# A first MLP matmul split into four full 128-row chunks and a paired half-array remainder, with the bias in the gelu

## The chip, the cores and the metric

The kernel runs on one core of one Trainium2 chip. The metric is device time in microseconds (us), of which lower is better. Before the change it was 450.98 us, the median of two runs (450.38 and 451.58).

Names: PE is TensorE, ACT is ScalarE, DVE is VectorE, POOL is GpSimd. A *tile* is 128 of the 2048 token rows, so there are 16. A *stage* is the first MLP matmul of one tile. The *pace* is the distance between the first matmuls of two successive stages, read from the timeline.

## The reference, cut to what matters

```python
# x: 2048 x 576, bf16; w1: 576 x 4608; w2: 4608 x 576
h  = x + attention(layernorm(x)) @ wo             # sliding, dilated, 8 keys a row
y  = layernorm(layernorm(h))
out = h + gelu(y @ w1 + b1) @ w2 + b2             # approximate (tanh) gelu
```

576 channels are four and a half blocks of 128. The change is about that half block.

## The kernel before

A front projects all 16 tiles to q, k, v; then, tile by tile, attention (mostly DVE), output projection (`pw`), layernorm, first MLP matmul (`pm`), gelu (ACT) and second MLP matmul (`po`) run as a pipeline. The first MLP uses five row blocks. The fifth holds the last 64 channels and, at row 64, the bias, met by a column of ones in the activations:

```python
ps_qkv = ... bufs=2, PSUM     # pq and pw
ps_m1  = ... bufs=3, PSUM     # pm: one bank is 4 blocks of 128 outputs, x 128 tokens, f32
# w1_sb[0:64, 4] = w1[512:576];  w1_sb[64, 4] = b1;  hn[:, 576] = 1, hn[:, 577:640] = 0
for g in range(g0, g1):                           # 9 groups a tile, one bank each
    pm = ps_m1.tile([P, GF, P], F32, tag="pm")
    for j in range(GF):
        ft = g * GF + j
        for kt in range(5):
            matmul(pm[:, j, :], lhsT=w1_sb[:, kt, ft*P:(ft+1)*P], rhs=hnT[:, kt, :], ...)
    nc.scalar.activation(out=hTg[:], in_=pm[:], func=Gelu_apprx_tanh)   # 128 x 512
# per iteration: E(it-2); G(it-3, 28..36); loads; F(it-2, first two thirds); C(it-1);
#                F(it-2, rest); D(it-1); G(it-2, 0..28); attention(it)
#                E: transposes hn; F: first MLP; C: transposes o; D: pw, layernorm; G: second MLP
```

The order of the source is not the order on the engines: the tile framework orders the instructions when it builds the program.

## Time and profile before

| stretch | what bounds it |
|---|---|
| 0 to 97 us | front: PE 94% busy and DMA share 0.96 from 56 to 90 us |
| 97 to 263 us | stages start 20.65 to 27.7 us apart; waits on attention and on ACT |
| 263 to 451 us | PE is full; one tile every 20.65 us |

From the page of the kernel before: engine totals, small DMA packets, the chain that ended last by engine, and two groups of instructions (count, busy us, mean ns of one, then idle time before and what ended it):

```profile
PE 408.3 (91%) x4752; PEld 338.5 (75%) x4752; DVE 293.5 (65%) x475; ACT 196.8 (44%) x307; POOL 49.2 (11%) x73
...
DMA packets 56072, 69.32 MB, mean 154 GB/s; under 512 B 2762, under 2 KB 53194, under 8 KB 55896
...
PE 58%; DVE 23%; issue 3%; ACT 2%; POOL 2%; DMA 1%; DVEq 0%; SPq 0%; ACTq 0%; POOLq 0%
...
L328 PE MATMUL pm<-hnT,w_sb 128*128 128x128 bf16 x2880 | 171.8, 222 | 10.1 <-ACT hTg L331 9.3
...
L331 ACT ACTIVATE hTg<-pm 128x512 bf16<-128x512 f32 x144 | 83.4, 598 | 65.5 <-PE pm L328 64.5
```

The gelu is 144 instructions of 598 ns and waits for PE. PE's 9.3 us of waiting for it all lie in the early tiles; from 263 us on there is none. The chain of waits in order of time (start, duration, what) in the late part of the kernel before holds only PE, and repeats every 20.65 us:

```profile
283.84 6.70 PE pm L328 x120
290.82 3.35 PE pm L328 x60
294.17 1.23 PE pw L299 x10
```

One such stage in the timeline of the kernel before (start, duration, engine, line, what; in brackets how long the engine had been idle and what ended that):

```profile
345.63 6.86 PE L328 MATMUL pm<-hnT,w_sb 128*128 128x128 bf16 x120
347.00 1.28 ACT L331 ACT_TABLE_LOAD   x1 [2.43 <-PE pm L328]
348.29 1.58 ACT L331 ACTIVATE hTg<-pm 128x512 bf16<-128x512 f32 x3
350.36 0.60 ACT L331 ACTIVATE hTg<-pm 128x512 bf16<-128x512 f32 x1 [0.50 <-PE pm L328]
...
352.61 3.51 PE L328 MATMUL pm<-hnT,w_sb 128*128 128x128 bf16 x60
...
355.96 1.39 PE L299 MATMUL pw<-wo_sb,oT 128*128 128x432 bf16 x10
```

From 345.63 to 355.96 PE never stops: 180 matmuls and five transposes, 55.8 ns from start to start (the 222 ns of the group is the modelled length of one pipelined matmul, not its cost). ACT is idle about half a microsecond before most gelus.

### The profile page before, as it was taken

To read this page: it belongs to the slowest core of one execution; us is meant where nothing else is said; L and a number is where in the kernel's file an instruction comes from. 1 tells how busy PE (TensorE), PEld (TensorE's weight loads), DVE (VectorE), ACT (ScalarE), POOL (GpSimd) and SP (SyncE) were. 2 spreads that over 40 slices of the span, in tenths; PEclk is the share of its full clock that TensorE was granted. 3 is DMA by queue.
4 is the path that set the end of the run, shared out by engine and by line. 5 is a ranking of instruction groups with operands and counts; after the bars stand their busy time and mean duration, and the time that the engine had idled before them with its cause. 6 is when DMAs were issued, how large, how long until landed. Compare 5 with 4: busy or idle time off the path is not lost.

```text
span 450.8 us, 10955 instructions
## 1 busy us (share of the span) xinstructions
PE 408.3 (91%) x4752; PEld 338.5 (75%) x4752; DVE 293.5 (65%) x475; ACT 196.8 (44%) x307; POOL 49.2 (11%) x73
## 2 busy tenths in 40 slices
PE   0898699849989996999878999999999999999996
PEld 0454355449878986798757898989898998989895
DVE  5835834941788998889997989787879772020200
ACT  5556366524272535072535443536263543324140
POOL 4310001010101010201030101010101101010100
PEclk9999699959999997999998999999999999999999
DMA  8497599999934735534734635334452000000000
GB/s 253 153 261 282 131 309 298 344 348 379 329 107 134 237 119 171 196 118 137 237 120 132 202 112 175 120 132 121 132 157 81 28 15 16 15 1 15 1 16 13
DMA packets 56072, 69.32 MB, mean 154 GB/s; under 512 B 2762, under 2 KB 53194, under 8 KB 55896
## 3 DMA queue, kind: packets, MB, share of 16 engines
q1 hardware_dynamic: 56024, 68.63, 47.7%
q8 instruction: 37, 0.61, 0.6%
q14 instruction: 11, 0.09, 0.1%
HBM read 59.13 MB, written 9.49 MB: 152 GB/s over the span
## 4 chain that ended last, share of the span: by engine, by line
PE 58%; DVE 23%; issue 3%; ACT 2%; POOL 2%; DMA 1%; DVEq 0%; SPq 0%; ACTq 0%; POOLq 0%
PE pm L328 26%; PE pq L203 5%; DVE prod L249 3%; PE pw L299 3%; DVE prod L252 2%; POOL ln_rstd L158 2%; DMA kw_758<-qkvd 1%; DVE prod L253 1%; DVE h L301 1%; PE po_1_6379 L347 1%; PE po_1_6028 L347 1%; PE po_0_5676 L347 1%; PE po_1_4955 L347 1%; PE po_0_4593 L347 1%; PE po_0_4232 L347 1%
## 5 line engine op out<-in xcount | busy, mean ns | idle before, releaser
L328 PE MATMUL pm<-hnT,w_sb 128*128 128x128 bf16 x2880 | 171.8, 222 | 10.1 <-ACT hTg L331 9.3
L328 PEld LDWEIGHTS <-w_sb 128*128 128x128 bf16 x2880 | 168.4, 100 | 12.3 <-issue 11.4
L347 PEld LDWEIGHTS <-hTg 128*128 128x128 bf16 x1152 | 111.7, 98 | 27.0
L331 ACT ACTIVATE hTg<-pm 128x512 bf16<-128x512 f32 x144 | 83.4, 598 | 65.5 <-PE pm L328 64.5
L203 PE MATMUL pq<-wqkv_sb,xnT 128*128 128x432 bf16 x320 | 65.8, 363 | 7.6 <-ACT qkv L205 6.8
L203 PEld LDWEIGHTS <-xnT 128*128 128x128 bf16 x320 | 31.8, 102 | 35.3 <-issue 11.8
L305 POOL TENSOR_TENSOR hb<-h,b_bc 128x576 bf16<-128x576 f32 x16 | 22.5, 1404 | 295.9 <-DVE h L301 295.9
L205 ACT CAST qkv<-pq 128x432 bf16<-128x432 f32 x64 | 32.9, 519 | 26.2 <-PE pq L203 20.6
L301 DVE TENSOR_TENSOR h<-pw,xr 128x432 f32<-128x432 f32 (+1 forms) x32 | 13.1, 450 | 41.9 <-PE pw L299 41.9
L166 ACT COPY hnT<-hnT_pt 128x640 bf16<-128x640 bf16 x16 | 11.0, 690 | 65.0 <-PE hnT_pt L165 65.0
L264 ACT ACTIVATE logits<-logits 128x256 f32<-128x256 f32 x16 | 6.7, 416 | 58.5 <-DVE logits L262 54.6
L158 POOL TENSOR_TENSOR ln_rstd<-ln_veps,mhalf 128x1 f32<-128x1 f32 x32 | 22.2, 694 | 69.7 <-DVE ln_veps L156 69.7
L331 ACT ACT_TABLE_LOAD x15 | 19.2, 1283 | 17.6 <-PE pm L328 17.5
L152 DVE BATCH_NORM_STATS2 ln_stats<-x_bf 128x6 f32<-128x288 bf16 x32 | 13.1, 446 | 17.4 <-DMA x_bf<-in_A_x_dram 17.3
L299 PE MATMUL pw<-wo_sb,oT 128*128 128x432 bf16 (+1 forms) x160 | 22.8, 290 | 1.0 <-ACT oT L166 0.9
L252 DVE TENSOR_TENSOR prod<-prod 128x2304 bf16<-128x2304 bf16 x16 | 22.4, 1400 | 0.4
L299 PEld LDWEIGHTS <-oT 128*128 128x128 bf16 x160 | 13.4, 99 | 8.5 <-ACT oT L166 1.4
L264 ACT ACT_TABLE_LOAD x14 | 18.0, 1283 | 2.0 <-DVE logits L262 1.8
L266 DVE TENSOR_REDUCE den<-logits 128x32 f32<-128x256 f32 x16 | 9.4, 588 | 10.6 <-ACT logits L264 10.6
L165 PE MATMUL xnT_pt<-ident,xn_84 128*128 128x128 bf16 x40 | 4.1, 242 | 11.8 <-DVE xn_84 L159 11.8
L165 PEld LDWEIGHTS <-xn_84 128*128 128x128 bf16 x40 | 3.2, 109 | 13.2 <-DVE xn_84 L159 11.8
L152 DVE BATCH_NORM_STATS2 ln_stats<-h 128x6 f32<-128x288 f32 x32 | 12.9, 447 | 0.0
(193 smaller groups left out, 589.9 us busy)
## 6 DMA issues: line engine op xcount, KB each, us to landing
w_sb<-in_B_w_dram SPq DMA_DIRECT2D x18, 576.0 KB, 8.1
qkvd<-qkv SPq DMA_DIRECT2D x16, 432.0 KB, 3.6
x_bf<-in_A_x_dram SPq DMA_DIRECT2D x16, 144.0 KB, 4.3
xr<-in_A_x_dram SPq DMA_DIRECT2D x16, 144.0 KB, 3.4
q<-qkvd SPq DMA_DIRECT2D x16, 144.0 KB, 4.9
out_dram<-o_sb SPq DMA_DIRECT2D x16, 144.0 KB, 1.7
wraw<-in_A_wqkv_dram SPq DMA_DIRECT2D x4, 432.0 KB, 3.5
kw_285<-qkvd SPq DMA_DIRECT2D x2, 576.0 KB
```

The source lines that it names most:

```text
L152: nc.vector.bn_stats(out=stats[:, c, :], in_=src[:, c * HALF:(c + 1) * HALF])
L158: nc.gpsimd.tensor_tensor(out=rstd[:], in0=veps[:], in1=mhalf[:], op=ALU.pow)
L203: nc.tensor.matmul(pq[:], lhsT=xnT[:, kt, :], rhs=wqkv_sb[:, kt, nq * QC:(nq + 1) * QC], start=(kt == 0), stop=(kt == KT - 1))
L205: nc.scalar.copy(out=qkv[:, nq * QC:(nq + 1) * QC], in_=pq[:])
L252: nc.vector.tensor_tensor(out=pv[:, :, 0:9, :], in0=pv[:, :, 0:9, :], in1=pv[:, :, 9:18, :], op=ALU.add)
L264: nc.scalar.activation(out=logits[:], in_=logits[:], func=ACT.Exp, scale=SCALE)
L299: nc.tensor.matmul(pw[:, 0:c1 - c0], lhsT=oT[:, kt, :], rhs=wo_sb[:, kt, c0:c1], start=(kt == 0), stop=(kt == KT - 1))
L301: nc.vector.tensor_tensor(out=h[:, c0:c1], in0=pw[:, 0:c1 - c0], in1=xr[:, c0:c1], op=ALU.add)
L305: nc.gpsimd.tensor_tensor(out=hb[:], in0=h[:], in1=b2_bc[:], op=ALU.add)
L328: nc.tensor.matmul(pm[:, j, :], lhsT=w1_sb[:, kt, ft * P:(ft + 1) * P], rhs=hnT[:, kt, :], start=(kt == 0), stop=(kt == KT - 1))
L331: nc.scalar.activation(out=hTg[:], in_=pm[:], func=ACT.Gelu_apprx_tanh)
L347: nc.tensor.matmul(po2[half][:], lhsT=hT[g][:, j, :], rhs=w2_sb[:, ft, half * HALF:(half + 1) * HALF], start=(ft == 0), stop=(ft == FT - 1))
```

## The change

The intent is to stop paying 36 full-array matmuls a tile for blocks that are half empty. The remaining 64 channels of two output blocks (`ft` and `ft + 18`) sit on partitions 0 to 63 and 64 to 127 and run side by side in the two halves of the array: 18 slots instead of 36. No row is left for the bias, so it becomes a per-partition operand of the gelu, which then needs one instruction for each 128-wide block. Halves that run together write to different banks (the Trainium skill, "TensorEngine Tiling (Array Packing)", section "Restrictions and Gotchas", says that different row tiles cannot use one PSUM bank at once), so a group now takes two of the three `pm` banks. The core of the diff, with cuts marked:

```diff
-    w1_sb = wpool.tile([P, KT, F], BF16, name="w1_sb")
+    w1_sb = wpool.tile([P, 4, F], BF16, name="w1_sb")
+    w1h_sb = wpool.tile([P, F2], BF16, name="w1h_sb")       # rows 512..575, two halves of F
+    b1_sb = wpool.tile([P, FT], F32, name="b1_sb")
+            nc.sync.dma_start(out=b1_bf[:], in_=B_b1.rearrange("(ft p) -> p ft", p=P))
+        nc.gpsimd.tensor_copy(out=b1_sb[:], in_=b1_bf[:])
     (w1 in 6 loads instead of 8; the double layernorm's eps folded in; hn's last 64 columns copied)
-            pm = ps_m1.tile([P, GF, P], F32, tag="pm", name="pm")
-            (4 blocks x 5 matmuls)
-            nc.scalar.activation(out=hTg[:], in_=pm[:], func=ACT.Gelu_apprx_tanh)
+            pms = [ps_m1.tile([P, GF, P], F32, tag="pm", name=f"pm{r}") for r in range(2)]
+            for j in range(n):
+                for r in range(2):
+                    matmul(pms[r][:, j, :], lhsT=w1h_sb[r*64:(r+1)*64, fa*P:(fa+1)*P],
+                           rhs=hnT[r*64:(r+1)*64, 4, :], start=(j == 0), stop=False, ...)
+            for r in range(2):
+                (4 blocks x 4 full matmuls into pms[r])
+            for r in range(2):
+                for j in range(GF):
+                    nc.scalar.activation(out=hTg[:, j, :], in_=pms[r][:, j, :],
+                                         func=ACT.Gelu_apprx_tanh, bias=b1_sb[:, ft:ft + 1])
```

More of the change, by code (lines that the diff above doesn't have):

```diff
@@ L41 @@
     FT = F // P
+    KC = 9
+    F2 = F // 2
+    FT2 = FT // 2
     NQ = 4
@@ L48 @@
     NG = FT // GF
+    NG2 = (FT2 + GF - 1) // GF
     LSK = 4
@@ L66 @@
     wo_sb = wpool.tile([P, KT, D], BF16, name="wo_sb")
-    w1_sb = wpool.tile([P, KT, F], BF16, name="w1_sb")
+    w1_sb = wpool.tile([P, 4, F], BF16, name="w1_sb")
+    w1h_sb = wpool.tile([P, F2], BF16, name="w1h_sb")
+    b1_bf = wpool.tile([P, FT], BF16, name="b1_bf")
+    b1_sb = wpool.tile([P, FT], F32, name="b1_sb")
     w2_sb = wpool.tile([P, FT, D], BF16, name="w2_sb")
@@ L127, in wo_load @@
         nc.sync.dma_start(out=wo_sb[64:128, KT - 1, :], in_=A_wo[0:64, :])
-    W1C = 8
+    W1C = 6
     CW = F // W1C
     def w1_chunk(c):
-        src = bass.AP(tensor=B_w1.tensor, offset=B_w1[0, c * CW].offset,
-                      ap=[[F, P], [P * F, 4], [1, CW]])
-        nc.sync.dma_start(out=w1_sb[:, 0:4, c * CW:(c + 1) * CW], in_=src)
+        w = F // W1C
+        src = bass.AP(tensor=B_w1.tensor, offset=B_w1[0, c * w].offset,
+                      ap=[[F, P], [P * F, 4], [1, w]])
+        nc.sync.dma_start(out=w1_sb[:, :, c * w:(c + 1) * w], in_=src)
     def w1_blk4():
-        nc.sync.dma_start(out=w1_sb[0:64, 4, :], in_=B_w1[512:576, :])
-        nc.sync.dma_start(out=w1_sb[64:65, 4, :], in_=B_b1.rearrange("(o f) -> o f", o=1))
-        nc.sync.dma_start(out=w1_sb[65:128, 4, :], in_=B_w1[0:63, :])
+        with nc.allow_non_contiguous_dma(reason="bias column layout"):
+            nc.sync.dma_start(out=b1_bf[:], in_=B_b1.rearrange("(ft p) -> p ft", p=P))
+        nc.gpsimd.tensor_copy(out=b1_sb[:], in_=b1_bf[:])
+        for r in range(2):
+            nc.sync.dma_start(out=w1h_sb[r * 64:(r + 1) * 64, :], in_=B_w1[512:576, r * F2:(r + 1) * F2])
     W2C = 9
@@ L155, in layernorm_to @@
         veps = pool.tile([P, 1], F32, tag=f"{tagp}_veps", name=f"{tagp}_veps")
-        nc.vector.tensor_scalar_add(out=veps[:], in0=mv[:, 1:2], scalar1=EPS)
+        if tagp == "ln2":
+            nc.vector.tensor_scalar(out=veps[:], in0=mv[:, 1:2], scalar1=1.0 + EPS, scalar2=EPS * EPS,
+                                    op0=ALU.mult, op1=ALU.add)
+        else:
+            nc.vector.tensor_scalar_add(out=veps[:], in0=mv[:, 1:2], scalar1=EPS)
         rstd = pool.tile([P, 1], F32, tag=f"{tagp}_rstd", name=f"{tagp}_rstd")
         nc.gpsimd.tensor_tensor(out=rstd[:], in0=veps[:], in1=mhalf[:], op=ALU.pow)
-        nc.vector.tensor_scalar(out=dst_bf[:, 0:D], in0=src, scalar1=mv[:, 0:1], scalar2=rstd[:, 0:1],
-                                op0=ALU.subtract, op1=ALU.mult)
+        if tagp == "ln2":
+            nc.vector.tensor_scalar(out=dst_bf[:, 0:D], in0=src, scalar1=mv[:, 0:1], scalar2=rstd[:, 0:1],
+                                    op0=ALU.subtract, op1=ALU.mult)
+            nc.vector.tensor_scalar(out=dst_bf[:, D:DP], in0=src[:, 512:D], scalar1=mv[:, 0:1],
+                                    scalar2=rstd[:, 0:1], op0=ALU.subtract, op1=ALU.mult)
+        else:
+            nc.vector.tensor_scalar(out=dst_bf[:, 0:D], in0=src, scalar1=mv[:, 0:1], scalar2=rstd[:, 0:1],
+                                    op0=ALU.subtract, op1=ALU.mult)
     def transpose_to(dstT, src_bf, tagp):
@@ L323, in stage_F @@
         for g in range(g0, g1):
-            pm = ps_m1.tile([P, GF, P], F32, tag="pm", name="pm")
-            for j in range(GF):
-                ft = g * GF + j
-                for kt in range(KT):
-                    nc.tensor.matmul(pm[:, j, :], lhsT=w1_sb[:, kt, ft * P:(ft + 1) * P], rhs=hnT[:, kt, :],
-                                     start=(kt == 0), stop=(kt == KT - 1))
-            hTg = sb.tile([P, GF, P], BF16, tag="hT", name="hTg", bufs=10)
-            nc.scalar.activation(out=hTg[:], in_=pm[:], func=ACT.Gelu_apprx_tanh)
-            d["hT"].append(hTg)
-        if g1 == NG:
+            pms = [ps_m1.tile([P, GF, P], F32, tag="pm", name=f"pm{r}") for r in range(2)]
+            n = min(GF, FT2 - g * GF)
+            for j in range(n):
+                fa = g * GF + j
+                for r in range(2):
+                    nc.tensor.matmul(pms[r][:, j, :], lhsT=w1h_sb[r * 64:(r + 1) * 64, fa * P:(fa + 1) * P],
+                                     rhs=hnT[r * 64:(r + 1) * 64, 4, :], start=(j == 0), stop=False,
+                                     skip_group_check=True)
+            for r in range(2):
+                for j in range(n):
+                    ft = r * FT2 + g * GF + j
+                    for kt in range(4):
+                        nc.tensor.matmul(pms[r][:, j, :], lhsT=w1_sb[:, kt, ft * P:(ft + 1) * P],
+                                         rhs=hnT[:, kt, :], start=False, stop=(kt == 3), skip_group_check=True)
+            for r in range(2):
+                hTg = sb.tile([P, GF, P], BF16, tag="hT", name="hTg", bufs=10)
+                for j in range(GF):
+                    fa = g * GF + j
+                    if fa >= FT2:
+                        break
+                    ft = r * FT2 + fa
+                    nc.scalar.activation(out=hTg[:, j, :], in_=pms[r][:, j, :], func=ACT.Gelu_apprx_tanh,
+                                         bias=b1_sb[:, ft:ft + 1])
+                    d["hT"].append((hTg, j, ft))
+        if g1 == NG2:
             d.pop("hnT")
@@ L344, in stage_G @@
         for ft in range(f0, f1):
-            g, j = ft // GF, ft % GF
+            hTg, j, fx = hT[ft]
             for half in range(2):
-                nc.tensor.matmul(po2[half][:], lhsT=hT[g][:, j, :], rhs=w2_sb[:, ft, half * HALF:(half + 1) * HALF],
+                nc.tensor.matmul(po2[half][:], lhsT=hTg[:, j, :], rhs=w2_sb[:, fx, half * HALF:(half + 1) * HALF],
                                  start=(ft == 0), stop=(ft == FT - 1))
@@ L366 @@
         nc.gpsimd.memset(o_slots[j][:, D:DP], 0.0)
-        nc.gpsimd.memset(hn_slots[j][:, D:D + 1], 1.0)
-        nc.gpsimd.memset(hn_slots[j][:, D + 1:DP], 0.0)
     emit_misc_setup()
@@ L396 @@
             pending.append((k, fn))
-    post = [lambda: w1_chunk(6), lambda: w1_chunk(7)] + [lambda c=c: w2_chunk(c) for c in range(W2C)] \
+    post = [lambda c=c: w2_chunk(c) for c in range(W2C)] \
         + [lambda: loads(2)]
@@ L420 @@
             loads(it + 1)
-        stage_F(it - 2, 0, 6)
+        stage_F(it - 2, 0, 3)
         stage_C(it - 1)
-        stage_F(it - 2, 6, NG)
+        stage_F(it - 2, 3, NG2)
         stage_D(it - 1)
```

## The prediction

> **What bounds the kernel now.** Three stretches. (1) Up to 97 us: the projection of all 16 tiles plus loading; the stretch table shows DMA share 0.96 from 56 to 90 us and 1.06 from 90 to 112 us. (2) From 97 us (first pm matmul) to about 247 us, MLP tiles start 20.7 to 27.8 us apart, the chain of waits mostly in VectorE's attention. (3) From 247 us on TensorE is full: the chain holds only PE, one tile every 20.65 us: 180 first-MLP matmuls (120 in 6.70 us, so 55.9 ns each, 10.05 us). The gelu there is cheap: the timeline shows 9 ACTIVATEs of 128x512 per tile, 598 ns each (0.49 us apart back to back).
>
> **What the change does.**
> - TensorE: 36 of the 180 matmuls of a tile become 36 half-array ones. If a pair shares one slot, 18 slots are saved: 18 x 55.9 ns = 1.0 us a tile, 16 us in all. That is an upper bound: the trace cannot show whether pairs overlap or what going from half to full array and back costs.
> - ScalarE: per tile 36 ACTIVATEs of 128x128 with a bias pointer replace 9 of 128x512 without. From the trace's 432, 512 and 640 wide PSUM reads (519, 598, 690 ns) the slope is about 0.83 ns an element, so a 128-wide one is about 280 ns; the Trainium skill, "ScalarE: Activation LUTs", section "What ACT_TABLE_LOAD costs", adds about 93 ns for each pointer operand (not in this trace). About 370 ns long, some 0.26 to 0.29 us apart: 9.4 to 10.6 us a tile against 4.5 to 5.4.
> - That lands inside the first-MLP stage. Only three pm banks exist, and now a group takes two, so group g+1 cannot start before the gelus of the bank it takes are done. ACT starts about 2.1 us after the stage's first matmul (table load 1.28 us after its first block) and must finish seven of ten banks before the last group runs. Estimate: 2.1 + 28 x 0.27 + 0.6 + about 1.2 = 11.5 us for the stage, against 10.05 + 0.44 (oT transposes) now. So the stage becomes ACT-bound and grows by about 1 us a tile (0 to 2), instead of shrinking by 1: about +17 us over 16 tiles.
> - Loading: the bias goes into columns, 4608 two-byte elements; by the Trainium skill, "DMA: Bandwidth & Descriptors", "Rules for kernel authors", a strided last dimension is one descriptor per element. At this trace's mean 61 ns a packet (47.7% of 16 engines' span over 56024 packets), 288 per engine take about 18 us of a busy queue, with qkv stores behind them. Idle DMA time (share 0.51 from 45 to 56 us) absorbs part. Estimate: +7 us before the first MLP matmul.
>
> **Predicted time:** 474 us, 8 in 10 between 450 and 498. Faster by over 2%: 0.07; within 2%: 0.20; slower by over 2%: 0.73.
>
> **What would show each step.** Gelu group about 370 ns x576; "PE pm waits for ACT hTg" growing from 9.3 us to 20 or more; tile pace after 250 us about 21.7 us instead of 20.65; half matmuls under 56 ns apart; over 4000 more small packets and a later first pm matmul.
>
> **What would make it wrong.** If the bias pointer costs nothing, ACT keeps pace and the pace falls to about 20 us: then 440 to 450. If pairs don't overlap, more is lost. The order around the early tiles' exp may change too.

## The result, and the profile after

The changed kernel took 470.1 us (median of 469.85 and 470.35) against 450.98: ratio 1.0431, 95% interval 1.0385 to 1.0476. A ratio here is the mean time of one kernel's fast runs over that of the other's of the same rounds, so it is not quite the ratio of the medians quoted.

The same parts of the page of the changed kernel:

```profile
PE 426.8 (91%) x4752; PEld 328.8 (70%) x4752; DVE 297.4 (64%) x491; ACT 267.0 (57%) x739; POOL 48.4 (10%) x70
...
DMA packets 59650, 68.77 MB, mean 147 GB/s; under 512 B 7360, under 2 KB 56768, under 8 KB 59598
...
PE 55%; DVE 12%; ACT 11%; issue 3%; POOL 2%; DVEq 0%; ACTq 0%; POOLq 0%
```

ACT went from 196.8 to 267.0 us busy and from 2% to 11% of the chain. The count of matmuls did not fall: 36 full ones a tile became 36 half ones. The late part of the chain, where before there was only PE:

```profile
309.56 1.01 PE pm_4620 L356 x16
310.64 1.28 ACT L365
312.20 0.89 ACT hTg L365 x3
313.51 1.00 PE pm_4673 L356 x16
315.66 0.62 PE pm_4724 L356 x9
316.37 1.15 ACT hTg L365 x4
317.94 1.00 PE pm_4784 L356 x16
318.94 0.89 PE pm_4785 L356 x16
321.44 1.23 PE pw L319 x10
```

Within one stage the chain now goes from PE to ACT and back: a bank of matmuls, the table load and gelus, the matmuls that could take the freed bank, gelus again. One group of the narrow gelus by its source line (count, then shortest, median and longest ns):

```profile
L365 ACT ACTIVATE hTg<-pm_1101,b_sb x4: 361/368/377, 101.5 to 102.3; 128x128 bf16<-128x128 f32 x4
```

And a stage in the timeline of the changed kernel:

```profile
354.24 0.23 PE L349 MATMUL pm_5402<-hnT,w1h_sb 64*128 64x128 bf16 x1
354.24 0.23 PE L349 MATMUL pm_5403<-hnT,w1h_sb 64*128 64x128 bf16 x1
354.30 0.22 PE L349 MATMUL pm_5402<-hnT,w1h_sb 64*128 64x128 bf16 x1
354.31 0.22 PE L349 MATMUL pm_5403<-hnT,w1h_sb 64*128 64x128 bf16 x1
...
354.42 0.22 PE L349 MATMUL pm_5403<-hnT,w1h_sb 64*128 64x128 bf16 x1
...
354.57 1.07 PE L356 MATMUL pm_5402<-hnT,w_sb 128*128 128x128 bf16 x16
...
356.46 0.39 PE L349 MATMUL pm_5454<-hnT,w1h_sb 64*128 64x128 bf16 x4
...
357.01 1.14 ACT L365 ACTIVATE hTg<-pm_5402,b_sb 128x128 bf16<-128x128 f32 x4
...
358.03 1.16 ACT L365 ACTIVATE hTg<-pm_5403,b_sb 128x128 bf16<-128x128 f32 x4
...
362.91 0.21 PE L349 MATMUL pm_5567<-hnT,w1h_sb 64*128 64x128 bf16 x1 [0.41 <-ACT hTg L365]
```

Three things are to be seen. Two halves start together (both at 354.24, the next pair 0.06 us later): pairs do share a slot. Between the last half (354.42) and the first full matmul (354.57) there are 0.15 us, not 0.06. And at 356.46 four halves of one bank run alone, although the source writes them in pairs, so there are more changes between half and full array than the source has. The builder placed them so; e4 and e11 below show why.

Where the 17.3 us between the two profiled spans (450.8 and 468.1) lie, by stage starts: the first stage begins at 97.73 us instead of 97.26 (+0.5); the ninth at 286.62 instead of 283.68 (+2.5 more over eight tiles, which had slack to give); the last at 443.98 instead of 428.25 (+12.8 over seven tiles); the rest is the tail (+1.6).

All start-to-start distances of a late stage, from its first matmul to the first `pw` matmul, can be sorted into four kinds. A full matmul or transpose costs 56 ns. A *trip* is a change from full to half array (152 ns start to start) and back (148 ns); what exceeds 56 ns there counts as "changes". What exceeds the usual distance is "wait". ("Full" is the count times 56 ns, so the row of the kernel before is 0.03 above its measured stage.) The same sum for the experiments below is in the table already, since it is what they are read by (us a tile):

| kernel | full | halves | changes | wait | stage | pace |
|---|---|---|---|---|---|---|
| before | 10.36 | - | - | 0 | 10.33 | 20.65 |
| changed | 8.34 | 1.75 | 1.41 | 0.62 | 12.12 | 22.54 |
| e1: one wide gelu per bank, no bias | 8.34 | 1.29 | 1.03 | 0.14 | 10.80 | 21.22 |
| e2: narrow gelus, no bias pointer | 8.34 | 1.40 | 1.03 | 0.23 | 11.01 | 21.42 |
| e3: before, with narrow gelus and pointer | 10.36 | - | - | 0.47 | 10.82 | 21.15 |
| e4: changed, five banks | 8.34 | 1.08 | 0.84 | 0.03 | 10.29 | 20.71 |
| e8: five banks, wide gelu, 3 trips | 8.34 | 1.05 | 0.47 | 0.01 | 9.87 | 20.29 |

The change saves 2.02 us of full matmuls a tile. Ideally the halves need 1.08 of that back; they take 1.75 because pairs are apart (of the 288 pairs in the whole trace, 61 start within 10 ns of each other; the expectation of e11 counts 207 as apart, so 81 together). Changes take 1.41 and waits 0.62. So PE loses in three ways, only one of them a visible wait. The question for the experiments is what makes the two others: the order as such, the narrow gelus, or the banks.

### The profile page after: what moved, and what is told of

It reads as the page before. It is cut to its first block, busy times and chain, and to the rows that moved or that the text cites. A ratio compares the mean times of both kernels' runs of the same rounds, so it can differ in the third digit from the quotient of the medians.

```text
span 468.1 us, 11416 instructions
## 1 busy us (share of the span) xinstructions
PE 426.8 (91%) x4752; PEld 328.8 (70%) x4752; DVE 297.4 (64%) x491; ACT 267.0 (57%) x739; POOL 48.4 (10%) x70
## 2 busy tenths in 40 slices
DMA packets 59650, 68.77 MB, mean 147 GB/s; under 512 B 7360, under 2 KB 56768, under 8 KB 59598
## 4 chain that ended last, share of the span: by engine, by line
PE 55%; DVE 12%; ACT 11%; issue 3%; POOL 2%; DVEq 0%; ACTq 0%; POOLq 0%
ACT hTg L365 7%; PE pw L319 4%; ACT L365 3%; DVE prod L269 2%; PE pq L223 2%; POOL ln_rstd L172 1%; DVE prod L272 1%; PE po_0_3719 L382 1%; PE po_0_6827 L382 1%; PE po_1_6447 L382 1%; PE po_0_5674 L382 1%; PE po_1_5284 L382 1%; PE po_0_4892 L382 1%; PE po_1_4502 L382 1%; PE po_1_4111 L382 1%
## 5 line engine op out<-in xcount | busy, mean ns | idle before, releaser
L356 PEld LDWEIGHTS <-w_sb 128*128 128x128 bf16 x2304 | 130.7, 98 | 13.0 <-issue 0.2
L223 PE MATMUL pq<-wqkv_sb,xnT 128*128 128x432 bf16 x320 | 65.6, 362 | 11.0 <-ACT qkv L225 10.3
L349 PEld LDWEIGHTS <-w1h_sb 64*128 64x128 bf16 x576 | 28.4, 94 | 24.8 <-issue 12.4
L272 DVE TENSOR_TENSOR prod<-prod 128x2304 bf16<-128x2304 bf16 x16 | 21.7, 1356 | 0.4
L162 DVE BATCH_NORM_STATS2 ln_stats<-x_bf 128x6 f32<-128x288 bf16 x32 | 13.4, 446 | 12.4 <-DMA x_bf<-in_A_x_dram 12.4
L273 DVE TENSOR_TENSOR prod<-prod 128x1024 bf16<-128x1024 bf16 x16 | 11.8, 735 | 0.4
```

Source lines behind the costliest of these rows:

```text
L162: nc.vector.bn_stats(out=stats[:, c, :], in_=src[:, c * HALF:(c + 1) * HALF])
L223: nc.tensor.matmul(pq[:], lhsT=xnT[:, kt, :], rhs=wqkv_sb[:, kt, nq * QC:(nq + 1) * QC], start=(kt == 0), stop=(kt == KT - 1))
L272: nc.vector.tensor_tensor(out=pv[:, :, 0:9, :], in0=pv[:, :, 0:9, :], in1=pv[:, :, 9:18, :], op=ALU.add)
L349: nc.tensor.matmul(pms[r][:, j, :], lhsT=w1h_sb[r * 64:(r + 1) * 64, fa * P:(fa + 1) * P], rhs=hnT[r * 64:(r + 1) * 64, 4, :], start=(j == ...
L356: nc.tensor.matmul(pms[r][:, j, :], lhsT=w1_sb[:, kt, ft * P:(ft + 1) * P], rhs=hnT[:, kt, :], start=False, stop=(kt == 3), skip_group_che ...
```

## The experiments

Theory A: ACT's 36 narrow gelus, holding three banks, bind the stage; torn pairs and extra trips are what the builder does when a partner's bank is not free. Rival B: PE itself is slower through half-array work. Rival D: the built order alone is at fault. The comparison with the reference passed for all, also for those without the bias, so it does not see this bias; those are called wrong.

### e1: one wide gelu per bank, no bias (wrong)

```diff
-                for j in range(GF): ... nc.scalar.activation(out=hTg[:, j, :], ..., bias=b1_sb[:, ft:ft + 1])
+                nc.scalar.activation(out=hTg[:, 0:n, :], in_=pms[r][:, 0:n, :], func=ACT.Gelu_apprx_tanh)
```

> The changed kernel with one 128x512 gelu per bank and no bias (the result is wrong on purpose), all matmuls kept. Theory A (the stage is bound by ScalarE's 36 narrow gelus and the banks they hold): the first-MLP stage falls from 12.06 to about 10.4 us, the late pace from 22.54 to about 20.7 us, the time to 446 to 456 us. It does not fall clearly below the kernel before, because each change between full and half array costs about 95 ns (full to half 151 ns against 56 ns start to start in the trace), 10 a tile or more. Rival B (TensorE itself is slower through these changes and broken pairs): stays above 463 us, pace above 22 us.

Measured: 455.39 us, ratio 1.0134 (1.0099 to 1.0169); pace 21.22 us. Most of the loss is gone, so ACT's part is real. What is left is hardly visible as a wait: PE waits 0.14 us a stage, but makes about 5.9 trips a tile and leaves 59 of 288 pairs torn. The time agrees with theory A; pace and stage (10.75 us from first to last matmul) are above its numbers. The trace shows where the rest sits. The stages at 21.22 us begin with ACT's table load of 1.28 us, so that the first gelu starts 2.77 us after the first matmul. The last tiles need no load, because no softmax comes between: there the first gelu starts at 1.49 us, PE makes 5 trips with all 18 pairs together, and the two last distances are 20.71 us. So in the late tiles wide gelus need more than three banks only behind a table load.

### e2: narrow gelus without the pointer (wrong)

```diff
-    nc.scalar.activation(..., func=ACT.Gelu_apprx_tanh, bias=b1_sb[:, ft:ft + 1])
+    nc.scalar.activation(..., func=ACT.Gelu_apprx_tanh)
```

> The changed kernel with its 36 narrow gelus a tile but no bias pointer (wrong on purpose). Theory A1 (it is the pointer operand's extra time): a gelu of 128x128 drops from about 365 to about 275 ns, 0.26 to about 0.17 us apart, so 36 take 6.1 us; stage about 10.7 us, pace about 21, time 450 to 458 us. Theory A2 (it is the count of instructions): stays 463 to 471 us.

Measured: 458.2 us, ratio 1.0204 (1.0159 to 1.025); pace 21.42 us. The group in its trace:

```profile
L365 ACT ACTIVATE hTg<-pm 128x128 bf16<-128x128 f32 x576 | 113.4, 290 | 42.3 <-PE pm L356 36.0
```

Back to back these gelus are 157 ns apart; in the changed kernel, with the pointer, 250 ns. The difference is 93 ns. The Trainium skill, "ScalarE: Activation LUTs", section "What ACT_TABLE_LOAD costs", gives about 93 ns for a pointer operand; this agrees (93 ns of spacing, and 90 ns of length after an idle ACT, 368 against 278). Of the 1.32 us of pace between the changed kernel and e1, the pointer is 1.12 and the count of instructions 0.20. Theory A1 holds; the time is just above its range.

### e3: the kernel before, with narrow gelus and the pointer

```diff
+    b1_bf, b1_sb loaded as in the change;  hn's column 576 = 0 instead of 1
-            nc.scalar.activation(out=hTg[:], in_=pm[:], func=ACT.Gelu_apprx_tanh)
+            for j in range(GF):
+                nc.scalar.activation(out=hTg[:, j, :], in_=pm[:, j, :], ..., bias=b1_sb[:, ft:ft + 1])
```

> The kernel before, matmuls and single-bank groups unchanged, only with the bias as a column and 36 narrow gelus with the pointer a tile. Theory A: ScalarE bounds the stage here too, stage about 11.1 us instead of 10.27, late pace about 21.5, time 456 to 464 us. If the narrow gelus harm only together with half-array matmuls or with groups of two banks: within 1% of before, 448 to 454 us.

Measured: 455.85 us, ratio 1.0159 (1.0115 to 1.0204); pace 21.15 us, later 20.65. Its gelus, with 458 ns as the mean because many are issued while the one before still runs:

```profile
L338 ACT ACTIVATE hTg<-pm,b_sb 128x128 bf16<-128x128 f32 x576 | 156.5, 458 | 17.2 <-PE pm L333 16.7 <-ACT hTg L338 0.3
```

So narrow gelus cost 0.5 us of wait a stage where a group holds one bank, and only in stages that begin with the table load (the two last distances, without it, are 20.65 us). The time is just below the range expected, the pace less than expected, and far from the 1.9 us of the change: the two-bank groups make it worse (the half-array work alone costs 0.06 us a tile where banks suffice, as e4 and e9 show).

### e4: the changed kernel with five banks

```diff
-    ps_qkv = ... bufs=2 ...;  ps_m1 = ... bufs=3
+    ps_m1 = ... bufs=5
-    pq = ps_qkv.tile(...);  pw = ps_qkv.tile(...)
+    pq = ps_m1.tile([P, QC], F32, tag="pm", padded_shape=[P, GF * P], ...);  pw likewise
```

> The changed kernel with one pool of five PSUM banks for all of pq, pw and pm (three for pm alone until now), nothing else changed. Theory A with banks as the channel: TensorE runs ahead while ScalarE finishes under the later stages; stage about 10.3 us, late pace 20.3 to 20.9 us, time 440 to 455 us. If banks are not what ties TensorE to ScalarE, or if half/full changes are the cost: 464 to 472 us.

Measured: 444.1 us, ratio 0.9877 (0.9841 to 0.9912). Nothing about the gelus changed and no bank was added to the total: two that served `pq` and `pw` are now shared. A stage in its timeline:

```profile
335.60 0.40 PE L348 MATMUL pm<-hnT,w1h_sb 64*128 64x128 bf16 x8
335.93 1.96 PE L355 MATMUL pm<-hnT,w_sb 128*128 128x128 bf16 x32
...
337.82 0.40 PE L348 MATMUL pm<-hnT,w1h_sb 64*128 64x128 bf16 x8
338.15 1.96 PE L355 MATMUL pm<-hnT,w_sb 128*128 128x128 bf16 x32
338.37 6.29 ACT L364 ACTIVATE hTg<-pm,b_sb 128x128 bf16<-128x128 f32 x24
...
345.89 1.39 PE L318 MATMUL pw<-wo_sb,oT 128*128 128x432 bf16 x10
```

PE runs its groups through, eight halves and 32 full ones at a time, while ACT works 24 gelus off in one stretch behind it, and ends after the stage, under the second MLP. So the narrow gelus cost only through the banks that they hold. PE is full again, and the pace is 20.71 us. This is not below the 20.65 us of the kernel before: where nothing holds PE back, the half-array work gains nothing.

### e5: the kernel before with five banks (control)

The same edit on the kernel before.

> Control: the kernel before with the same pool of five PSUM banks for pq, pw and pm. Its late pace is TensorE-bound already, so it stays 20.65 us; the front and the early tiles lose some waits, as they did in the changed kernel with five banks (its first MLP matmul 92.5 us against 97.7, early tiles). Expected 438 to 446 us, so within 1% of the changed kernel with five banks (444.1): then the half-array change is worth nothing even where ScalarE no longer holds it back. If the half-array matmuls do pay: 3 to 4% slower than that, 456 us or more.

Measured: 445.89 us, ratio 0.9908 (0.9871 to 0.9945); pace 20.65 us as before. The first stage begins at 92.97 us (92.52 in e4). The gain of e4 over the kernel before is thus that of the shared banks in the front and the early tiles; the intervals of e4 and e5 overlap.

### e6, e8 and e9: the price of a trip

In e6 (five banks, otherwise the change) each group is cut in two rounds of halves, then full matmuls: 10 trips a tile instead of 5. In e8 and e9 (both five banks, wide gelu, no bias, wrong) the halves of two groups are done together (e8, 3 trips) or not (e9, 5 trips).

```diff
e6:
+            for js in (range(0, n // 2), range(n // 2, n)):   # halves and full matmuls of js only
e8:
-        for g in range(g0, g1): (halves of g; full matmuls of g; gelus of g)
+        for gs in ([g0, g0 + 1], [g0 + 2]) ...:  (halves of all gs; then full matmuls and gelu of each)
```

> The changed kernel with five banks, every group cut in two rounds of half-array then full-array matmuls: the same matmuls, nine returns from half to full array a tile plus one (10 trips instead of 5). If a trip costs 0.19 us (full to half +95 ns, half to full +92 ns): stage 10.24 to about 11.2 us, late pace 20.71 to about 21.65 us, time 455 to 462 us. If the gaps at the changes are only a reading of the profiler or are caught up later: pace stays 20.7, time 441 to 447 us.

> The changed kernel with five banks, one gelu per bank without bias (wrong on purpose), and the half-array matmuls of two groups done together: 3 trips a tile instead of 5. If a trip costs 0.19 us: stage about 9.9 us, late pace about 20.33 us, 5 to 7 us less than the same kernel with 5 trips. If not: the same as that one within 1 us.

> The 5-trip partner of the run before: five banks, one gelu per bank without bias (wrong on purpose). ScalarE no longer bounds the stage with five banks, so the late pace stays 20.71 us; time 438 to 445 us, up to 5 us below the same with narrow gelus because of the early tiles. If narrow gelus still cost there: 430 us or less.

| run | trips a tile | us, median | ratio (95% interval) | pace |
|---|---|---|---|---|
| e6 | 10 | 456.14 | 1.0137 (1.0102 to 1.0172) | 21.77 |
| e4 | 5 | 444.1 | 0.9877 (0.9841 to 0.9912) | 20.71 |
| e9 | 5 | 444.91 | 0.9894 (0.9853 to 0.9935) | 20.71 |
| e8 | 3 | 442.9 | 0.9834 (0.9784 to 0.9885) | 20.29 |

Five more trips cost 1.06 us of pace and two fewer save 0.42, so a trip costs 0.21 us both ways; 0.19 of it is the two longer distances. The Trainium skill, "TensorEngine Tiling (Array Packing)", section "Key Properties", says that changing the tiling mode drains TensorE, without a figure; the runs agree that it costs, and give one. The halves save 2.02 - 1.08 = 0.94 us a tile and five trips take 5 x 0.19 = 0.94 back. That is why the change gains nothing even with five banks. e9 against e4 also shows that with five banks wide and narrow gelus make no difference beyond the intervals. e8's total fell by only 2 us against e9, less than the 5 to 7 expected, although each late tile gained 0.42: the first eight distances took 183.7 us against 182.3, so in the early tiles the gain was lost to other waits. The total does not carry the claim; the pace does.

So rival B is right in part. Of the 1.89 us a tile that the change lost, 1.32 go with the narrow gelus (22.54 to 21.22, e1), 0.51 with the extra trips, torn pairs and small waits that three banks still bring (21.22 to 20.71, e9), and 0.06 are the half-array work as the source writes it (20.71 against 20.65). The shares depend on the order of these steps: with the banks given first, e4 alone takes away 1.83 and the wide gelus then nothing. Narrow gelus and short banks cost only together, and 0.51 of the loss needs the table load too (e1).

### e11 and e12: the order pinned

Three banks again. Every first-MLP matmul is tied behind the matmul before it in the source, so that the builder cannot reorder them among themselves. It can still put other work between them.

```diff
-    nc.tensor.matmul(pms[r][:, j, :], ...)
+    tc.keep_in_program_order(nc.tensor.matmul(pms[r][:, j, :], ...))
```

> The changed kernel (three banks, 36 narrow gelus with the pointer) with the first-MLP matmuls pinned on TensorE in the order in which the source writes them: all half-array matmuls side by side, 5 trips a tile, where the changed kernel's built order has 7.75 trips and 207 of 288 pairs apart. Theory A (ScalarE and three banks bind the stage; the built order only fills the wait): the time saved on trips and pairs comes back as waits for gelus; stage 11.6 to 12.2 us, late pace 22.1 to 22.7, time 464 to 474 us. Rival D (the built order itself cost the 1.4 us): waits stay 0.6 us, stage 10.9 us, pace about 21.3, time 450 to 458 us.

> The same pinned order with one wide gelu per bank and no bias (wrong on purpose). With ScalarE out of the way three banks suffice: stage 10.3 to 10.5 us, late pace 20.7 to 20.9, time 446 to 453 us. If three banks bind even so: stage 10.8 us or more, as in the unpinned run with wide gelus.

e11 took 470.24 us, ratio 1.0463 (1.0429 to 1.0498), against 1.0431 for the change. Its pace over the last seven distances is 22.33 us, against 22.48. So the pin did not give the order that was asked for: a late stage has 9 stretches of halves instead of 5, since in four of its groups the builder put other matmuls between the first half and its partner, and 14 of 18 pairs run together. The totals therefore do not decide on rival D. The traces do. The lines are from the second groups of the same stage (the fourteenth, which needs no table load), first in the changed kernel, whose stage began at 399.59, then in e11, where it began at 400.38:

```profile
401.08 1.14 ACT L365 ACTIVATE hTg<-pm_6174,b_sb 128x128 bf16<-128x128 f32 x4 [2.66 <-PE pm_6174 L356]
...
401.81 0.34 PE L349 MATMUL pm_6226<-hnT,w1h_sb 64*128 64x128 bf16 x3
...
402.27 0.21 PE L349 MATMUL pm_6227<-hnT,w1h_sb 64*128 64x128 bf16 x1
```

```profile
401.88 2.18 ACT L366 ACTIVATE hTg<-pm,b_sb 128x128 bf16<-128x128 f32 x8 [2.66 <-PE pm L356]
...
402.60 0.23 PE L349 MATMUL pm<-hnT,w1h_sb 64*128 64x128 bf16 x1
...
402.76 0.29 PE L185 MATMUL oT_pt<-ident,o 128*128 128x128 bf16 x2
...
403.07 0.38 PE L349 MATMUL pm<-hnT,w1h_sb 64*128 64x128 bf16 x7
```

In both the fourth gelu ends 2.64 us after the stage's first matmul, and the first half for the bank that it frees starts at 2.68 and 2.69 us (402.27 and 403.07); in the next two groups it is 5.35 and 5.36, then 8.03 and 8.03. PE did different things before these moments and got no further in either, and the stage is 11.70 us in the one and 11.75 in the other. So here the gelus and the banks set the pace, and the torn pairs and single halves were work that PE did in time that it would otherwise have spent waiting: rival D falls for such a stage. The source's own order with three banks and these gelus was never run. (In the other tiles pinning let the builder move `po` matmuls into the stage, so its stage length is not comparable there; the pace is.)

e12 (wide gelu, wrong) took 461.97 us, ratio 1.0281 (1.024 to 1.0322), far above the 446 to 453 expected, and tells little. Its pace alternates between 20.71, as expected, and about 23.5. In the slow tiles the builder had put the softmax's exp, with its table load, into the stage:

```profile
339.28 1.28 ACT L284 ACT_TABLE_LOAD   x1
...
343.02 1.28 ACT L361 ACT_TABLE_LOAD   x1
...
344.96 0.27 PE L349 MATMUL pm<-hnT,w1h_sb 64*128 64x128 bf16 x3 [1.58 <-ACT hTg L361]
```

Between the two loads ACT is not at gelus, and PE waits for a bank. So the expectation failed through a side effect of pinning. The tiles at 20.71 do not prove it right either: each follows such a slow tile, or comes last, and needs no table load of its own, and without a load e1 has 20.71 unpinned.

### e7: only the load of the bias

```diff
+        nc.sync.dma_start(out=b1_bf[:], in_=B_b1.rearrange("(ft p) -> p ft", p=P))
+        nc.gpsimd.tensor_copy(out=b1_sb[:], in_=b1_bf[:])          # in the kernel before; never read
```

> The kernel before plus the load of the bias into columns and its cast (nothing reads them), issued where the changed kernel issues them. The prediction's step (some 18 us of queue time, +7 us before the first MLP matmul): first pm matmul at 102 us or later, time 454 to 460 us. Rival, from the changed kernel's trace (bias cast about 11 us after the issue, first MLP matmul at 97.7 us against 97.3 us): the load is absorbed; first pm matmul 96 to 99 us, time within 1% of before.

Measured: 454.56 us, ratio 1.0089 (1.004 to 1.0138); first stage at 100.85 us. This lies between the two: the time is at the low end of the first range, the first stage below it. Alone, the load delays it by some 3.6 us, read from one profile each; e3, which has the same load, begins at 99.00 us, so this is no better than 2 to 4 us. Its page:

```profile
DMA packets 60696, 69.33 MB, mean 153 GB/s; under 512 B 7386, under 2 KB 57818, under 8 KB 60520
...
q1 hardware_dynamic: 60648, 68.64, 47.9%
```

There are 4624 more packets under 512 B than before, as the Trainium skill's "DMA: Bandwidth & Descriptors", section "Rules for kernel authors", has it for a strided last dimension: one descriptor an element. But their time is tiny: 47.9% of 453.0 us against 47.7% of 450.8 us is 2 us an engine, not 18 (3 us when the packets of at most 4 bytes are summed in the two traces, some 10 ns each). What it costs is delay: in the timeline the cast of the bias starts 11 us after the load was issued (23.20 to 34.19 us). In the changed kernel the first stage came only 0.5 us late; it also loads 0.55 MB less (68.77 against 69.32 MB), in other pieces. Which of these made up for the rest was not separated.

### e10: a correct kernel with 3 trips and wide gelus

The channels of a normalised row sum to zero. So channel 575 can be replaced by a constant 1 whose weight row is the bias, if w1's row 575 is subtracted from the other rows, on the chip, while the front runs. Then no gelu needs a pointer.

```diff
+        nc.sync.dma_start(out=w575[:], in_=B_w1[575, c * w:(c + 1) * w].partition_broadcast(P))
+        eng.tensor_tensor(out=blk, in0=blk, in1=w575[:], op=ALU.subtract)     # every row block of w1
+    hn[:, 575] = hn[:, 639] = 1;  w1h_sb[63] and [127] = b1;  gelu and trips as in e8, five banks
```

> A correct kernel with 3 trips, one wide gelu per bank without pointer, and five banks: because the normalised channels of a row sum to zero, channel 575 is replaced by a constant 1 whose weight row is the bias, and w1's row 575 is subtracted from the other rows on the chip while the front runs[...]. If trips and pointer gelus are the two costs: late pace 20.29 us as in the 3-trip run; time 438 to 447 us, depending on what the subtraction adds to the front. If it is no better than the kernel before with five banks (445.9): the weight preparation eats the 0.36 us a tile.

Measured: 454.31 us, ratio 1.0091 (1.0055 to 1.0126). The late pace is 20.29 us, as foreseen. But the first stage begins at 107.61 us instead of 93.24 in e8. Its waits of PE (what waits, for what, us in total, times, longest) show why:

```profile
PE hnT_pt L190 <- DVE hn L179: 16.3, 3, 12.1
```

The subtraction (10.1 us on DVE, 16.2 on POOL in the timeline) delays the first attention and layernorm by more than 16 tiles of 0.36 us return. The version that beats both kernels stays the shared five banks, with the change (444.1) or without it (445.89); the latter is the simpler one.

## Why the prediction was right or wrong, point by point

- **The time** (474 predicted, 470.1 measured) and the direction were right. The sum was helped by luck. The stage term was foreseen as about 1 us in each of 16 tiles, +17 us; late tiles lost 1.9 us each, but the first eight only 2.5 us together, so that stages and tail came to 16.8 us of the 17.3. What remained of the miss is the load, +7 foreseen and 0.5 measured.
- **What bounds the kernel**: right. The early tiles hid most of the added work (+2.5 us over eight tiles), the late ones none.
- **The gain on TensorE, at most 1.0 us a tile**: right as a bound, and pairs do share a slot (3 to 4 ns between starts where they run together). The prediction named the change between full and half array without a size. The runs size it: 0.21 us a trip, which takes the whole gain at five trips.
- **ScalarE**: right in mechanism and size. 367 to 369 ns a gelu that follows an idle ACT, 250 ns apart back to back; predicted 370 and 260 to 290. e2 shows the pointer to be most of it.
- **"So the stage becomes ACT-bound and grows by about 1 us a tile"**: the mechanism was right (e1, e2 and e4 each undo most of the loss, e11 undoes none), the term too small: 12.06 us instead of the predicted 11.5, pace 22.54 instead of 21.7. The part that was short is ACT's start: the first gelu begins 2.77 us after the first matmul, not 2.1. The 28th gelu ends at 11.02 us where the first three terms of the estimate give 10.3, and the last matmul starts 1.04 us after that (about 1.2 foreseen).
- **The sign "PE pm waits for ACT hTg growing from 9.3 us to 20 or more"**: wrong. In the changed trace PE waits 2.2 us for gelus before halves, and 12.4 us of weight-load idle time is labelled "issue". The builder had ordered other work into the waits. And the list counts idle time only from the modelled end of a matmul, some 220 ns after its start, so short waits do not show in it: the tenth stage has distances of 345, 345 and 251 ns where 152, 56 and 152 are usual, and none of the three is listed. The loss shows in the pace and in the chain of waits, not in the list of waits.
- **"+7 us before the first MLP matmul"**: wrong. It was 0.5 us here and some 2 to 4 us alone (e3, e7). The failing term was 61 ns a packet: a mean over packets of over 1 KB does not hold for two bytes, which took 2 to 3 us of engine time in all.

## What to carry to other kernels

Cost a half-array remainder by its trips, not by its slots: here a change to half array and back costs 0.21 us, nearly as much as four full matmuls of 128 columns, so collect the halves of many groups or leave the array full. When a change moves work to the engine that empties PSUM, count the banks as well as its busy time: the same narrow gelus with their pointer cost 3.0% of the time with three banks (ratio 1.0431 against 1.0134 in e1, some 13 us) and nothing with five (0.9877 in e4, 0.9894 in e9). A table load at the start of the stage counts with the gelus, since the banks must cover it. And read a stage that got longer by its start-to-start distances, because an instruction order built around a shortage hides the wait.

## What the Trainium skill lacked or had wrong

- "TensorEngine Tiling (Array Packing)", "Key Properties": it says that a mode change drains TensorE but not what that costs. The runs show 152 ns start to start from full to half and 148 ns back, instead of 56 (0.21 us a trip by pace, e6 and e8). Its speedup table has no term for it.
- "ScalarE: Activation LUTs": its 93 ns for a pointer operand holds (250 against 157 ns apart). Overlap back to back is given as about 93 ns; here gelus of 598 ns were 478 or 494 ns apart, which is 104 to 120 ns, and the narrow ones overlap by about 118 (368 ns long, 250 apart) and 121 ns (278 long, 157 apart).
- "DMA: Bandwidth & Descriptors": its rule says one descriptor an element and gives no time; what the page has on small descriptors is an overhead in cycles and bytes, not the time of such a load. 4608 elements of two bytes took 2 to 3 us of each engine's time but 11 us from issue to use (e7).
- No page says that the instruction order a framework builds can hide a PSUM shortage, so that the waits listed shrink while the stage grows (9.3 us of waits before; 2.2 us after, with 1.9 us a tile lost).
